# Attention and two mixtures of products on one core: base addresses of TensorE's operands moved by 32 bytes, and a new searched order

## The chip, the cores and the metric

One core of a Trainium2 chip runs the whole kernel as one program. The metric is the device time of that program in microseconds; shown are the median of several runs and, beside it, one profiled execution. The matmul engine is called PE in the profile, its weight loads PEld, VectorE DVE, ScalarE ACT, GpSimd POOL, and SyncE, which issues the DMAs, SP.

## The reference

Three stages follow each other. Everything is float32.

```python
# attention, B=4, H=8, S=576, D=64; key blocks of 64, block-causal
scores = where(block(i) >= block(j), q @ k.T / sqrt(D), -1e9)
attn   = exp(scores - max) ; attn /= attn.sum(-1) + 1e-9
x      = (attn @ v)                      # -> 2304 tokens x 512
# first mixture: 512 -> 1536 -> 512
xn = x / sqrt(mean(x*x) + 1e-6) * rms_g
x  = (silu(xn @ w_gate) * (xn @ w_val)) @ w_out
# second mixture: 8 experts, 512 -> 1024 -> 512
P  = exp(x @ gate - max), 8 rounds of row and column normalising
out = sum over e of P[:, e] * (relu(x @ w1[e]) @ w2[e])
```

## The kernel before, in words

**Products.** Nearly every product is made of three fp32r matmuls: each factor is split into a rounded part (`hi`, written by a copy) and the rest (`lo`, written by a subtraction), and hi·hi, hi·lo and lo·hi are added in PSUM (`THREE`). In a call `matmul(lhsT, rhs)` the stationary factor is `lhsT`, loaded as 128 columns, and the moving one is `rhs`, of up to 512 columns. In the rows of the trace a matmul is written `out<-moving,stationary`, so `ps<-xs,w` streams `xs` past weights from `w`.

**Stages.** In the first 500 us the 32 heads of attention are interleaved with the first mixture's products on the first three of five token blocks (`moe1`, `groups`). Some 12 heads (`NEW`) work with transposed scores, the other 20 turn their probabilities on PE (`tr`, 15 transposes a head, with `ident` moving and `p` stationary). Then the middle pass (`middle`) does token blocks 3 and 4 with 7 products in the place of 8 (Strassen's way, `up`), 384 columns wide. The first pass of the second mixture (`first_pass`) takes 10 of 18 token tiles, as pieces of 384 and 256 columns, the second pass (`second_pass`) the other 8 as one piece of 512. In the second pass each of 16 groups has 2 x 42 products with `xs` moving (`up`) and 84 with a tile of `h` or `x` moving (`down2`).

**Where operands lie.** SBUF tiles are laid one after another, each in a multiple of 32 bytes of a partition. The pool `cst` on the left begins with `ident` (512 bytes), `ones` (512) and `rgs` (16, rounded up to 32); by that all that follows (`acc`, the weights `w`, `raw`, `h`, `t`, the two big `x`) begins at 32 bytes modulo 64. On the right the pool `att` of attention (`qa`, `qb`, `ka`, `kb`, `vs`, `p`, `pth`, `ptl` and others) holds 78,624 bytes up to byte 229,344, so it begins at 150,720: its operands lie at 0 modulo 64. When the first tile of the later stages is wanted, `late` (L1166) closes that pool and opens `c1` in its place: seven operand tiles `xs`, the scratch tile `pad`, `gwr`, `onec`, the routing tables. Each is made when it is first asked for while instructions are written out, and this pool too begins at 150,720, so `xs` and `pad` lie at 0 modulo 64. All slices taken of these tiles begin at multiples of 64 bytes from the tile's start. `cst` ends at 150,688, so 32 bytes lie unused between them.

**Order.** Nothing is written in program order. `G.op` records each operation with an engine, a planned duration, buffers and a priority; `emit` (L136) plans them on a model of the engines forward and backward `ROUNDS` times, then `move` (L158) adds noise to the keys of stretches of the planned line, one stretch for each seed in `MOVES`, starting below position `SPAN`. What comes out is the order of each engine's queue. `MARGIN` is added to the time at which a finished operation is seen by other engines. Some operations can be given to a second engine (`alts`). `replay` (L268) finds gaps on PE and fills them with small matmuls of `ident` on itself (`Array.fill`, L84).

**Places the change touches.** Constants L24 to L337; `Loader.convert` (L486, two ACT operations); the pool `att` (L515 on); `att_init` (L564) with a memset of `ones` (L566) that releases PE's 32 warm-up products, and memsets of mask tiles (L578, L600); `att_load` (L622), `s_d` (L731), `s_norm` (L853, L858); `late` (L1166); the set `PRE` (L1273), which has the same nine members before and after.

Of the kernel before, what the change touches and what calls it, by code (L numbers as in the profile page):

```python
# [9 lines left out]
F32 = mybir.dt.float32  # L10
F32R = mybir.dt.float32r
I32 = mybir.dt.int32
U32 = mybir.dt.uint32
# [8 lines left out]


GAIN, GAIN2 = 1500.0, 3000.0  # L24
ROUNDS = 7


class Buf:
# [72 lines left out]
class Graph:  # L101
# [222 lines left out]

BEGIN = {"ACT": 700.0, "DVE": 900.0, "PE": 0.0, "POOL": 700.0, "SP": 740.0}
SEEN = {"ACT": 140.0, "DVE": 115.0, "POOL": 110.0, "PE": 210.0}
MARGIN, LAND, RATE = 0.0, 2000.0, 300.0
DELAY, BYTES = 1760.0, 307.0
FILL, EMPTY = 0.8, 220.0
MOVES = (  # L330
# [5 lines left out]
)  # L336
SPAN = 4502  # L337


def transfers(dur):  # L340
# [10 lines left out]
def t_act(n, psum=False, ap=0):  # L351
    return (50 if psum else 92) + n / 1.2 + 90 * ap
# [31 lines left out]
def tile_attn_moe_moe2(ctx: ExitStack, tc: tile.TileContext, qT, kT, vP, wg, wv, wo, rg, gw, w1, w2, ident_d, mq_d, mk_d, bm_d, out):  # L384
# [14 lines left out]
    def f32(ap):  # L399
        return ap.bitcast(F32)  # L400
# [60 lines left out]
    class Loader:  # L461
# [24 lines left out]
        def convert(self, src, raw, prio):  # L486

            wd, y, up = WIDE.next(), CVT[0].next(), CVT[1].next()

            def part(dt, i):  # L490
                return wd().bitcast(dt).rearrange("p (n w) -> p n w", w=2)[:, :, i]

            def i32(b):
                return b().bitcast(I32)

            ops = [
                G.op("SP", 2200, lambda: nc.sync.dma_start(out=wd().bitcast(U64), in_=src), w=[wd], prio=prio, lat=2000),

                G.op("ACT", t_act(512), lambda: nc.scalar.activation(out=y(), in_=part(F32, 1), func=AF.Prelu, scale=2.0**-112, alpha=2.0**32),
                     r=[wd], w=[y], prio=prio),  # L500
                G.op("ACT", t_act(512), lambda: nc.scalar.activation(out=i32(up), in_=part(U32, 0), func=AF.Copy, scale=2.0**-29),
                     r=[wd], w=[up], prio=prio),
                G.op("DVE", t_v2(512), lambda: nc.vector.tensor_scalar(
                    out=i32(y), in0=i32(y), scalar1=3, scalar2=None, op0=ALU.logical_shift_left), r=[y], w=[y], prio=prio),
                G.op("POOL", t_pool(512), lambda: nc.gpsimd.tensor_tensor(out=i32(raw), in0=i32(y), in1=i32(up), op=ALU.add),
                     r=[y, up], w=[raw], prio=prio),
            ]
            self.conv += ops
# [16 lines left out]
    PP = [Ring(tiles(att, 2, [128, 128 * (t + 1)], F32, f"p{t}_")) for t in range(5)]  # L525
    PTH = Ring(tiles(att, 2, [128, 512], F32R, "pth"))
    PTL = Ring(tiles(att, 2, [128, 512], F32R, "ptl"))
    MN = Ring(tiles(att, 2, [128, 6], F32, "mn"))
    SM = Ring(tiles(att, 2, [128, 5, 3], F32, "sm"))
    RS = Ring(tiles(att, 2, [128, 5], F32, "rs"))  # L530
    XX = Ring(tiles(att, 5, [128, S], F32, "xx"))
    SS = Ring(tiles(att, 1, [128, S], F32, "ss"))
    CL = Ring(tiles(att, 1, [128, 5], F32, "cl"))
    TM = Ring(tiles(att, 3, [128, S], F32, "tm"))
    guard, zeros = fixed(None), fixed(None, par=True)
    masks = {}

# [25 lines left out]

    def att_init():  # L564

        A("DVE", 200, lambda: nc.vector.memset(ones_t, 1.0), w=[ones], prio=-2.0)  # L566
        pt, first = PO.next(), RS.next()

        def warm():
            for _ in range(16):  # L570
                pe.matmul(out=pt()[:, 0:128], lhsT=ones_t, rhs=ones_t, start=True, stop=True)

        A("PE", 6800, warm, r=[ones], w=[pt], prio=-2.0)
        A("ACT", 1500, lambda: nc.scalar.activation(out=first()[:, 0:1], in_=ones_t[:, 0:1], func=AF.Exp), r=[ones], w=[first], prio=-2.0)
        m = [RQ0.next(), RQ0.next()]
        for b, src, ring, o in ((m[0], mq_d, QB0, PAD), (m[1], mk_d, KB0, 0)):
            def fill(b=b, one=ring is KB0):
                nc.vector.memset(b()[64:128], 0.0)  # L578
                if one:
                    nc.vector.memset(b()[96:106], 1.0)  # L580

            def rows(b=b, src=src):
                nc.sync.dma_start(out=b()[64:68], in_=src[0:4])
                nc.sync.dma_start(out=b()[68:72, PAD:S], in_=src[0:4, 0 : S - PAD])

            A("DVE", 1300 if ring is KB0 else 650, fill, w=[b])
            A("SP", 1150, rows, w=[b], lat=2000)
            for t in ring.tiles:
                masks[id(t)] = m_ = fixed(t, par=True)
                copy(A, S, lambda t=t, o=o: t[64:128, o : o + S], lambda b=b: b()[64:128], r=[b], w=[m_])  # L590
        A("SP", 300, lambda: nc.sync.dma_start(out=bm_t, in_=bm_d), w=[bm], lat=2000)
        for t in VX.tiles:
            A("POOL", 400, lambda t=t: nc.gpsimd.memset(t[:, :, 0:D], 1.0), w=[vones])
            A("POOL", 180, lambda t=t: nc.gpsimd.memset(t[0:64, 4, :], 0.0), w=[vones])
        for t in SM.tiles:
            A("DVE", 60, lambda t=t: nc.vector.memset(t, 0.0), w=[guard])
            A("DVE", 60, lambda t=t: nc.vector.memset(t[:, :, 1], 1e-9), r=[guard], w=[guard])
        for t in (*QA0.tiles, *QB0.tiles):
            m_ = masks.setdefault(id(t), fixed(t, par=True))
            A("DVE", 75, lambda t=t: nc.vector.memset(f32(t[:, 0:PAD]), 0.0), w=[m_])  # L600
        for t in range(5):
            for p in PP[t].tiles:
                A("POOL", 80, lambda t=t, p=p: nc.gpsimd.memset(p[:, NKEY[t] :], 0.0), w=[zeros])

    def att_load(i):
# [13 lines left out]
        if PLAIN <= i < PLAIN + 2:  # L619

            clear = st["clear", i % 2] = qb.part()
            A("DVE", 300, lambda: nc.vector.memset(f32(qb()[96:128, :]), 0.0), w=[clear])  # L622
        qq, kk = Rrq.next(), Rrq.next()
        load_two(kk, kT)
        load_two(qq, qT)
# [99 lines left out]
    def s_d(i):  # L725
        ps2, ps, m = st.pop(("s2", i)), ps_ring[0].next(), st["m", i]
        s_mm(i, ps, 0, 4, 512, 64)
        s_min(i, ps, 0, 5, 64)
        both = Buf(m.get)
        both.writes, both.before = set(m.writes), set()  # L730
        A("DVE", 70, lambda: nc.vector.tensor_scalar(  # L731
            out=m()[:, 4:5], in0=m()[:, 4:5], scalar1=m()[:, 5:6], scalar2=None, op0=ALU.min),
          w=[both], r=[m])
        m.writes |= both.writes
        m.users |= both.writes
        s_exp(i, ps2, 0, 4, 0, 0, 512)
        s_exp(i, ps, 0, 4, 512, 2, 64)
        if i in NEW:
            spread_max(i, ps)
# [104 lines left out]
    def s_norm(i):  # L844
        if i in NEW:
            return
        P, sm, r = st["P", i], st["sm", i], RS.next()

        def recip():
            nc.vector.tensor_reduce(out=r(), in_=sm(), axis=AX, op=ALU.add)  # L850
            nc.vector.reciprocal(out=r(), in_=r())

        A("DVE", 400, recip, r=[sm], w=[r])  # L853
        st["Pn", i] = []
        for t in range(5):
            n, p = NKEY[t], P[t]
            q = Buf(p.get)
            A("ACT", t_act(n), lambda t=t, n=n, p=p: nc.scalar.activation(  # L858
                out=p()[:, 0:n], in_=p()[:, 0:n], func=AF.Copy, scale=r()[:, t : t + 1]), r=[r, p], w=[q],
              alts=[("DVE", Both(63 + t_v2(n)), lambda t=t, n=n, p=p: nc.vector.tensor_scalar_mul(  # L860
                  out=p()[:, 0:n], in0=p()[:, 0:n], scalar1=r()[:, t : t + 1]))], margin=500.0)
            p.users |= q.users
            q.users = p.users
            st["Pn", i].append(q)
# [300 lines left out]

    def late(make):  # L1166

        box = []

        def get():  # L1170
            if not c_pool:
                att_stack.close()
                c_pool.append(ctx.enter_context(tc.tile_pool(name="c1", bufs=1, side="right", reuse_waits="tile")))
            if not box:
                box.append(make(c_pool[0]))
            return box[0]

        return get

    def late_buf(make, par=False):  # L1180
        b = Buf(late(make), par=par)
# [88 lines left out]
                    out=dst(), in0=ps()[:, 0:n], in1=dst(), op=ALU.add), r=[ps, dst], w=[dst])  # L1270

    kept, folded = {}, {}
    PRE = {('g', 1), ('g', 4), ('v', 1), ('g', 0), ('g', 3), ('v', 0), ('g', 5), ('v', 2), ('g', 2)}  # L1273

    def join(r, w, prio):
        hi, lo = (lambda: f32(w()[:, 0, :])), (lambda: f32(w()[:, 1, :]))
# [763 lines left out]
```

## Time and profile before

| | us |
|---|---|
| median of 3 runs (2166.33 to 2170.77) | 2166.95 |
| the profiled execution, its own time | 2168.07 |
| its span, first to last instruction | 2166.3 |
| PE busy | 2141.8 (99%) |
| PE weight loads | 1839.4 (85%) |
| DVE, POOL, ACT busy | 1510.9, 1192.0, 958.3 |

A matmul's record is longer than the time after which the next one starts, since they are pipelined; so the pace of PE is read from starts: a row of the timeline merges consecutive instructions of one kind, and its start subtracted from the start of the row behind it, divided by the count, is the pace. Busy time over count, in the groups by line, is close to it but counts the overlap once.

### The profile page before, as it was taken

Reading aid. Unit: us, or ns where it says so; the run is one execution under the profiler, and the core shown is the slowest. Engines: PE = TensorE matmul, PEld = TensorE weight load, DVE = VectorE, ACT = ScalarE, POOL = GpSimd, SP = SyncE. Lnnn points to the kernel's source line nnn. Section 1 sums busy time; section 2 is a strip of 40 time slices with the busy share of each in tenths; the row PEclk is TensorE's granted clock in tenths of the full one; section 3 lists DMA queues with packets and bytes.
Section 4 is the critical chain, followed back from the end, with each engine's and each line's share of the span. In section 5 each row is a group of like instructions: output and inputs, shape, how many; then the busy total and the mean of one; then the engine's idle time right before and its main releaser. Section 6 shows DMA issues by size and latency. Waiting matters only on the chain.

```text
span 2166.3 us, 31299 instructions
## 1 busy us (share of the span) xinstructions
PE 2141.8 (99%) x10924; PEld 1839.4 (85%) x10924; DVE 1510.9 (70%) x2576; ACT 958.3 (44%) x2055; POOL 1192.0 (55%) x1083
## 2 busy tenths in 40 slices
PE   8899999999999999999999999999999999999999
PEld 6777888888999889898999999989888888888887
DVE  8778886677556786666666656666767676776767
ACT  5668785663434434333333333433433233332332
POOL 4576424558436655555555555553655464564644
PEclk9999999999999999999999999999999999999999
DMA  5667754557654645555555544444766556565553
GB/s 170 204 209 240 240 181 155 178 183 268 236 170 148 214 176 201 187 185 188 182 182 183 177 178 175 175 177 163 238 199 209 181 194 208 190 211 188 194 197 114
DMA packets 166914, 414.39 MB, mean 191 GB/s; under 512 B 26378, under 2 KB 61642, under 8 KB 166756
## 3 DMA queue, kind: packets, MB, share of 16 engines
q1 hardware_dynamic: 166756, 412.39, 56.3%
q8 instruction: 86, 1.41, 0.3%
q14 instruction: 72, 0.59, 0.1%
HBM read 261.24 MB, written 150.53 MB: 190 GB/s over the span
## 4 chain that ended last, share of the span: by engine, by line
PE 91%; DVE 4%; ACT 3%; DMA 1%; issue 1%; POOL 0%; SPq 0%; ACTq 0%; DVEq 0%; POOLq 0%
PE pm L94 53%; PE ps L94 30%; PE po L94 5%; PE ps L98 1%; ACT p L858 1%; ACT p L697 1%; DVE mn L690 1%; PE pm L88 0%; ACT pth L874 0%; DMA kv<-w 0%; ACT tm L933 0%; DMA acc<-tm 0%; DVE ptl L875 0%; DMA w<-ko 0%; ACT w L443 0%
## 5 line engine op out<-in xcount | busy, mean ns | idle before, releaser
L94 PE MATMUL ps<-xs,w 128*128 128x384 f32 (+2 forms) x2613 | 536.3, 349 | 0.8 <-DVE pad L1501 0.8
L94 PEld LDWEIGHTS ps<-xs,w 128*128 128x128 f32 x2613 | 462.0, 188 | 54.4 <-DVE pad L1501 1.9
L94 PE MATMUL pm<-x,w 128*128 128x512 f32 (+2 forms) x1743 | 420.3, 375 | 2.0 <-DVE t L1244 1.1
L94 PEld LDWEIGHTS pm<-x,w 128*128 128x128 f32 x1743 | 306.8, 189 | 50.4 <-DVE t L1246 1.3
L1783 DVE SCALAR_TENSOR_TENSOR acc<-pm,Pm,acc 128x512 f32<-128x512 f32 x280 | 209.3, 748 | 114.9 <-PE pm L94 114.8
L94 PE MATMUL pm<-w,h 128*128 128x512 f32 x1152 | 280.4, 391 | 0.0
L456 POOL TENSOR_TENSOR w<-raw,w 128x512 fp32r<-128x512 f32 (+1 forms) x150 | 192.9, 1288 | 154.5 <-ACT w L443 143.8
L94 PE MATMUL pm<-h,w 128*128 128x512 f32 (+1 forms) x1068 | 248.6, 378 | 0.2 <-ACT x L443 0.2
L94 PEld LDWEIGHTS pm<-w,h 128*128 128x128 f32 x1152 | 209.7, 188 | 39.1
L94 PEld LDWEIGHTS pm<-h,w 128*128 128x128 f32 x1068 | 194.3, 188 | 30.1 <-ACT t L1496 0.6
L94 PE MATMUL pm<-w,x 128*128 128x512 f32 x768 | 192.8, 393 | 0.0
L1501 DVE TENSOR_TENSOR pad<-ps,pad 128x384 f32<-128x384 f32 (+2 forms) x154 | 81.2, 528 | 121.5 <-ACT pad L1496 87.1
L94 PEld LDWEIGHTS pm<-w,x 128*128 128x128 f32 x768 | 140.9, 188 | 24.9
L1496 ACT ACTIVATE pad<-ps 128x384 f32<-128x384 f32 (+2 forms) x142 | 68.1, 480 | 184.6 <-PE ps L94 183.5
L94 PE MATMUL pm<-xs,w 128*128 128x256 f32 (+2 forms) x699 | 149.7, 338 | 0.0
L1907 DVE TENSOR_TENSOR acc<-pm,acc 128x512 f32<-128x512 f32 x169 | 115.8, 686 | 45.2 <-PE pm L94 41.4
L443 ACT ACTIVATE w<-raw 128x512 fp32r<-128x512 f32 (+1 forms) x179 | 105.2, 590 | 91.6 <-PE pm L94 38.6
L94 PEld LDWEIGHTS pm<-xs,w 128*128 128x128 f32 x699 | 120.0, 188 | 16.7 <-DVE x L1738 0.4
L456 POOL TENSOR_TENSOR w<-pad,w 128x512 fp32r<-128x512 f32 x62 | 84.8, 1388 | 67.5 <-ACT w L443 41.6
L456 POOL TENSOR_TENSOR x<-pad,x 128x512 fp32r<-128x512 f32 (+1 forms) x74 | 99.8, 1352 | 32.8 <-ACT x L443 30.9
L94 PE MATMUL ps<-x,w 128*128 128x256 f32 (+1 forms) x627 | 114.3, 303 | 0.0
L456 POOL TENSOR_TENSOR h<-pad,h 128x512 fp32r<-128x512 f32 (+1 forms) x51 | 67.9, 1340 | 71.4 <-ACT h L443 43.3
(382 smaller groups left out, 3866.8 us busy)
## 6 DMA issues: line engine op xcount, KB each, us to landing
raw<-w_dram SPq DMA_DIRECT2D x128, 256.0 KB, 3.5
w<-ko SPq DMA_DIRECT2D x36, 512.0 KB, 4.5
w<-kv SPq DMA_DIRECT2D x33, 512.0 KB, 4.7
fa<-w SPq DMA_DIRECT2D x32, 512.0 KB, 2.6
fc<-w SPq DMA_DIRECT2D x32, 512.0 KB, 3.5
fd<-w SPq DMA_DIRECT2D x32, 512.0 KB, 3.1
sb<-w SPq DMA_DIRECT2D x32, 512.0 KB, 4.3
sd<-pad SPq DMA_DIRECT2D x32, 512.0 KB, 2.6
```

What stands on the lines that cost most here:

```text
L94: return self.tensor.matmul(**k)
L98: return self.tensor.transpose(**k)
L443: nc.scalar.activation(out=out_(), in_=in_(), func=AF.Copy, scale=scale)
L456: eng.tensor_tensor(out=out_(), in0=a(), in1=b(), op=ALU.subtract)
L690: return A("DVE", t_v1(n), lambda: nc.vector.tensor_reduce(out=m()[:, col : col + 1], in_=ps()[:, o : o + n], axis=AX, op=ALU.max, negate= ...
L697: A("ACT", t_act(n, True, 2), lambda: nc.scalar.activation(out=p()[:, c0 : c0 + n], in_=ps()[:, o : o + n], func=AF.Exp, bias=m()[:, t : t ...
L858: A("ACT", t_act(n), lambda t=t, n=n, p=p: nc.scalar.activation(out=p()[:, 0:n], in_=p()[:, 0:n], func=AF.Copy, scale=r()[:, t : t + 1]), ...
L1496: G.op("ACT", t_act(n, True), lambda: nc.scalar.activation(out=t()[:, 0:n], in_=bank()[:, 0:n], func=AF.Copy), r=[bank], w=[t])
L1501: G.op("DVE", t_v1(n), lambda: nc.vector.tensor_tensor(out=t()[:, 0:n], in0=bank()[:, 0:n], in1=t()[:, 0:n], op=ALU.add), r=[bank, t], w=[t])
L1783: G.op("DVE", 63 + t_v1(512), lambda y=y, dst=dst, tt=tt, e=e: nc.vector.scalar_tensor_tensor(out=dst(), in0=wide(y()), scalar=Pm()[:, tt, ...
L1907: G.op("DVE", t_v1(N), lambda: nc.vector.tensor_tensor(out=dst(), in0=bank()[:, 0:N], in1=dst(), op=ALU.add), r=[bank, dst], w=[dst])
```

## The change

Four things are changed together. The pool of attention gets one more tile of 32 bytes and, with that, its tiles `xx`, `ss`, `tm` stand ahead of the small ones. The late pool's tiles are all made at its opening, in a fixed order (`xs` 0 to 6, `pad`, `onec`, then `gwr`, `lg`, then the rest), and a tile of 32 bytes is added. Both pools thus hold 32 bytes more, and fill the 32 bytes that were free. Planned durations, `MARGIN` and `ROUNDS` are changed, and the list of moves is another, so the order on every engine is another. In `att_init` the memsets of masks are made to come behind the memset of `ones`.

```diff
-ROUNDS = 7
+ROUNDS = 9
-MARGIN, LAND, RATE = 0.0, 2000.0, 300.0
+MARGIN, LAND, RATE = 60.0, 2000.0, 300.0
 MOVES = (
...
-SPAN = 4502
+SPAN = 3975
...
-                G.op("ACT", t_act(512), lambda: nc.scalar.activation(out=y(), ...
+                G.op("ACT", 45 + t_act(512), lambda: nc.scalar.activation(out=y(), ...
-                G.op("ACT", t_act(512), lambda: nc.scalar.activation(out=i32(up), ...
+                G.op("ACT", 45 + t_act(512), lambda: nc.scalar.activation(out=i32(up), ...
...
     PTL = Ring(tiles(att, 2, [128, 512], F32R, "ptl"))
+    XX = Ring(tiles(att, 5, [128, S], F32, "xx"))
+    SS = Ring(tiles(att, 1, [128, S], F32, "ss"))
+    TM = Ring(tiles(att, 3, [128, S], F32, "tm"))
     MN = Ring(tiles(att, 2, [128, 6], F32, "mn"))
     SM = Ring(tiles(att, 2, [128, 5, 3], F32, "sm"))
     RS = Ring(tiles(att, 2, [128, 5], F32, "rs"))
-    XX = Ring(tiles(att, 5, [128, S], F32, "xx"))
-    SS = Ring(tiles(att, 1, [128, S], F32, "ss"))
     CL = Ring(tiles(att, 1, [128, 5], F32, "cl"))
-    TM = Ring(tiles(att, 3, [128, S], F32, "tm"))
+    att.tile([128, 8], F32, name="even")
...
-        A("DVE", 200, lambda: nc.vector.memset(ones_t, 1.0), w=[ones], prio=-2.0)
+        begun = {A("DVE", 200, lambda: nc.vector.memset(ones_t, 1.0), w=[ones], prio=-2.0)}
...
-            A("DVE", 1300 if ring is KB0 else 650, fill, w=[b])
+            A("DVE", 1300 if ring is KB0 else 650, fill, w=[b], after=begun)
...
-            A("DVE", 75, lambda t=t: nc.vector.memset(f32(t[:, 0:PAD]), 0.0), w=[m_])
+            A("DVE", 75, lambda t=t: nc.vector.memset(f32(t[:, 0:PAD]), 0.0), w=[m_], after=begun)
...
-            A("DVE", 300, lambda: nc.vector.memset(f32(qb()[96:128, :]), 0.0), w=[clear])
+            A("DVE", 750, lambda: nc.vector.memset(f32(qb()[96:128, :]), 0.0), w=[clear])
...
-        A("DVE", 70, lambda: nc.vector.tensor_scalar(
+        A("DVE", 135, lambda: nc.vector.tensor_scalar(
...
-        A("DVE", 400, recip, r=[sm], w=[r])
+        A("DVE", 300, recip, r=[sm], w=[r])
...
-            A("ACT", t_act(n), lambda t=t, n=n, p=p: nc.scalar.activation(
+            A("ACT", t_act(n, ap=1), lambda t=t, n=n, p=p: nc.scalar.activation(
...
     def late(make):
-        box = []
+        k = len(lates)
+        lates.append(make)
         def get():
             if not c_pool:
                 att_stack.close()
                 c_pool.append(ctx.enter_context(tc.tile_pool(name="c1", bufs=1, side="right", reuse_waits="tile")))
-            if not box:
-                box.append(make(c_pool[0]))
-            return box[0]
+                for i in (*range(2, 11), 0, 1, *range(11, len(lates))):
+                    lates[i] = lates[i](c_pool[0])
+                c_pool[0].tile([128, 8], F32, name="odd")
+            return lates[k]
         return get
+    lates = []
```

## Rows read from the trace of the kernel before

**Rows 1.** The page: share of the chain that ended last, by engine.

```profile
PE 91%; DVE 4%; ACT 3%; DMA 1%; issue 1%; POOL 0%; SPq 0%; ACTq 0%; DVEq 0%; POOLq 0%
```

**Rows 2.** Windows, first 500 us: length, busy of PE, PEld, DVE, ACT, POOL, clock, DMA.

```profile
0.00:60.00 60.00, 51.92 (x249) 39.80 (x249) 49.26 (x120) 36.01 (x75) 29.18 (x43) 0.91 0.60 172
60.00:125.00 65.00, 58.19 (x306) 47.87 (x307) 46.72 (x105) 43.05 (x98) 40.55 (x36) 0.95 0.58 176
125.00:250.00 125.00, 122.39 (x625) 97.48 (x624) 108.27 (x226) 95.13 (x231) 78.66 (x67) 1.00 0.76 244
250.00:500.00 250.00, 248.48 (x1309) 205.87 (x1308) 188.86 (x430) 164.98 (x423) 114.14 (x105) 1.00 0.58 187
```

**Rows 3.** Timeline of PE, second pass: start, length, form, count.

```profile
1709.40 2.88 PE L94 MATMUL pm<-x,w 128*128 128x512 f32 x12
1712.12 1.56 PE L94 MATMUL ps<-xs,w 128*128 128x512 f32 x6
...
1750.83 7.16 PE L94 MATMUL ps<-xs,w 128*128 128x512 f32 x30
1757.82 1.56 PE L94 MATMUL pm<-xs,w 128*128 128x512 f32 x6
```

**Rows 4.** Timeline of PE, first pass.

```profile
1058.28 5.42 PE L94 MATMUL ps<-xs,w 128*128 128x384 f32 x30
1063.54 1.55 PE L94 MATMUL pm<-w,x 128*128 128x512 f32 x6
```

**Rows 5.** Timeline of PE, middle pass.

```profile
596.11 7.44 PE L94 MATMUL pm<-h,w 128*128 128x384 f32 x42
603.39 1.20 PE L94 MATMUL ps<-x,w 128*128 128x384 f32 x6
...
608.60 1.20 PE L94 MATMUL ps<-xs,w 128*128 128x384 f32 x6
609.64 1.20 PE L94 MATMUL pm<-xs,w 128*128 128x384 f32 x6
```

**Rows 6.** Groups of PE by line and form, whole span: count, busy us, mean ns, idle.

```profile
L94 PE MATMUL ps<-xs,w 128*128 128x384 f32 x1383 | 262.0, 338 | 0.2 <-DVE pad L1501 0.2
L94 PE MATMUL ps<-xs,w 128*128 128x512 f32 x846 | 207.6, 395 | 0.0
...
L94 PE MATMUL pm<-xs,w 128*128 128x512 f32 x270 | 70.3, 395 | 0.0
...
L94 PE MATMUL ps<-xs,x 128*128 128x512 f32 x162 | 41.0, 395 | 0.0
...
L94 PE MATMUL pm<-xs,w 128*128 128x384 f32 x141 | 29.1, 339 | 0.0
...
L94 PE MATMUL pm<-xs,x 128*128 128x512 f32 x66 | 17.2, 396 | 0.0
```

**Rows 7.** Timeline of all engines, first 10 us.

```profile
3.00 0.17 DVE L566 MEMSET ones<- 128x128 f32 x1
...
3.22 5.88 PE L94 MATMUL po<-ones 128*128 128x128 f32 x32 [3.22 <-DVE ones L566]
...
7.25 0.75 DVE L640 TENSOR_TENSOR qa<-rq,qa 64x576 fp32r<-64x576 f32 x1
...
8.86 0.45 PE L94 MATMUL ps<-ka,qa 128*128 128x448 f32 x1
```

**Rows 8.** Timeline of all engines, the change from attention's tiles to the late pool.

```profile
521.16 1.43 DVE L1072 SCALAR_TENSOR_TENSOR acc<-xx,rgs,ss 128x64 f32<-128x64 f32 x3
521.27 1.05 POOL L1377 TENSOR_TENSOR pad<-acc,acc 128x384 f32<-128x384 f32 x1
...
542.28 1.32 PE L94 MATMUL ps<-x,w 128*128 128x384 f32 x6
```

**Rows 9.** Groups of PE by line and form, 0 to 500 us alone.

```profile
L94 PE MATMUL pm<-x,w 128*128 128x512 f32 x744 | 200.7, 403 | 2.0 <-DVE t L1244 1.1 <-DVE t L1246 0.8
```

**Rows 10.** One line's instructions: count, duration in ns as minimum, median, maximum.

```profile
L731 DVE TENSOR_SCALAR mn<-mn x32: 196/210/218, 13.9 to 465.4; 128x1 f32<-128x1 f32 x32
```

More of the change, by code (lines that the diff above doesn't have):

```diff
@@ L497, in convert @@
                 G.op("SP", 2200, lambda: nc.sync.dma_start(out=wd().bitcast(U64), in_=src), w=[wd], prio=prio, lat=2000),
-                G.op("ACT", t_act(512), lambda: nc.scalar.activation(out=y(), in_=part(F32, 1), func=AF.Prelu, scale=2.0**-112, alpha=2.0**32),
+                G.op("ACT", 45 + t_act(512), lambda: nc.scalar.activation(out=y(), in_=part(F32, 1), func=AF.Prelu, scale=2.0**-112, alpha=2.0**32),
                      r=[wd], w=[y], prio=prio),
-                G.op("ACT", t_act(512), lambda: nc.scalar.activation(out=i32(up), in_=part(U32, 0), func=AF.Copy, scale=2.0**-29),
+                G.op("ACT", 45 + t_act(512), lambda: nc.scalar.activation(out=i32(up), in_=part(U32, 0), func=AF.Copy, scale=2.0**-29),
                      r=[wd], w=[up], prio=prio),
@@ L1272, in tile_attn_moe_moe2 @@
     kept, folded = {}, {}
-    PRE = {('g', 1), ('g', 4), ('v', 1), ('g', 0), ('g', 3), ('v', 0), ('g', 5), ('v', 2), ('g', 2)}
+    PRE = {('g', 1), ('g', 4), ('g', 0), ('g', 3), ('v', 2), ('g', 2), ('v', 1), ('g', 5), ('v', 0)}
     def join(r, w, prio):
```

12 rows, old and new, of the table MOVES are left out of this document.

## The prediction

> **What bounds the kernel now.** I read the chain of waits first. The reader is to see that PE is 91% of the chain that ended last and no other engine has more than 4% [rows 1]: an instruction of PE that starts sooner brings the end nearer, anything else counts only where PE stands still. Where it does so is read from the windows. In the first 500 us PE is idle for 8.1, 6.8, 2.6 and 1.5 us, 19.0 in all [rows 2]; over the whole span it is 24.5 us (2166.3 less the 2141.8 of the table), so little is behind that. From 500 us on the time is the sum of the paces of PE's matmuls, so I read paces next, as starts in the timeline subtracted and divided by the count. In the second pass 12 products with `x` moving take 1712.12 - 1709.40 = 2.72 us, or 226.7 ns each; 30 with `xs` moving take 6.99 us, or 233.0 ns [rows 3]. Shape, weights and stage are the same. What differs is that `x` and `w` begin at 32 bytes modulo 64 and `xs` at 0, so that the moving and the stationary operand are of different classes in the second case. The same holds more weakly at 384 columns: 30 of `xs` in the first pass take 5.26 us, 175.3 ns [rows 4], 42 of `h` in the middle pass 7.28 us, 173.3 ns; but six of `xs` there take 1.04 us, also 173.3 ns [rows 5].
>
> **The change part by part.**
>
> *The late pool's base.* Before, it holds 78,624 bytes below byte 229,344; with 32 more it begins at 150,688, which is 32 modulo 64, and 8192 and 18432, the sizes of `xs` and `pad`, keep that class. All operands of the later passes are then of the class of `w`, `x` and `h`. The matmuls with `xs` moving and 512 columns number 846 + 270 + 162 + 66 = 1344 [rows 6]. If they go from 233.0 to 226.7 ns, 1344 x 6.3 = 8.5 us go, all from a stretch in which PE never waits, so all of it from the end. For 384 columns there are 1383 + 141 = 1524 [rows 6]. All at 2.0 ns would be 3.0 us; at the pace of the six in the middle pass it is nothing. I take 2.0 us, since two thirds or so of the 1524 lie in the first pass, where the slower pace was read. Products of 256 columns and the scratch operands in `pad` I leave at nothing, as no row parts them from the others. **-10.5 us**, between -11.5 and 0.
>
> *A rule that speaks against it.* The trace has 233.0 against 226.7 ns for the two classes [rows 3]. The Trainium skill, in "TensorE: Matmul & The Clock Gate", section "Step-by-step: what each phase is for", says that PE has two independent read ports into SBUF, one for the moving operand and one for weights, so that loading the next weights takes no bandwidth from the running matmul. By that rule the two bases could not collide, this term would be 0 and the time some 10.5 us longer. By the row I keep the term; the rule, taken at its word, is a rival below.
>
> *Attention's base.* Its operands move together from 0 to 32, so pairs within attention stay of one class; pairs at switches to and from products on `x` or `h`, mixed now, become equal, and the transposes, equal now, become mixed, since `ident` stays at 0 and `p` moves. No row isolates either. Bounds from the 6.3 ns of [rows 3]: some 200 switches give at most 1.3 us, 15 transposes in 20 heads lose at most 300 x 6.3 = 1.9 us. They stand against each other: **0**, between -1.3 and +1.9.
>
> *The memset of `ones` ahead.* Now DVE does five other memsets first; `ones` comes at 3.00 us, PE's warm-up starts at 3.22 us, runs for 5.88 us, and attention's first product starts right at its end, at 8.86 us [rows 7]. With `ones` first the warm-up is over up to 1.9 us sooner. What is late next is `qa`, whose split ends on DVE at 7.25 + 0.75 = 8.00 us [rows 7]. The memsets put behind cost DVE the 0.17 us of `ones` at most. **-0.7 us**, between -1.9 and 0.
>
> *The order of the late pool's tiles.* `pad` now lies over attention's `xx`, `ss` and `tm`, which are read last. The release waits on DVE: POOL's first write of `pad` at 521.27 us would wait until DVE's last reads of `xx` and `ss` end at 522.59 us [rows 8], 1.3 us, and POOL's folding of weights, queued behind it, with it. The first product that needs operands made through `pad` starts at 542.28 us [rows 8]. These 20 us, in which PE works on pending products of the first mixture, hide it: **0**; were that cover gone, 1.3 us.
>
> *The new order.* Removed and added instructions: none; each queue's order is another, in the first 500 us above all, SP's and POOL's included. One row says in which direction: the operation of L731, on the path from scores to exponentials, takes 210 ns 32 times [rows 10], and was planned with 70, now with 135. A plan that knows more of what the chip takes, and keeps 60 ns in hand at each handover, should stall less. What there is to win has two rows: the 19.0 us of idle [rows 2], of which 3.2 are the wait for `ones`, and the pace of the first mixture's products on `x` where attention is mixed in, 200.7 / 744 = 269.8 ns against 226.7, or 744 x 43.1 = 32 us [rows 9, 3]. Most of that slow pace is the price of switching to small products and back, which any order pays. What there is to lose is as large: an order can as well double the idle time. Between -15.8 (all idle but the wait for `ones`) and +19.0 (idle doubled) I take **-3.0 us**, near the small end, as both orders come from the same kind of search.
>
> **Sum.** -10.5 + 0 - 0.7 + 0 - 3.0 = -14.2 us. It stands against the profiled execution's own 2168.07 us, 1.8 us of which lie around the span: 2153.9 us. That execution is 1.1 us above the median of 2166.95 us, so the median should go to **2152.8 us**.
>
> **Rivals.**
>
> *The bases do nothing.* Either the ports are as separate as the cited rule has them and `xs` is slow for another reason, say because it lies highest in SBUF or is written while it is read; or the pool's base is rounded to 64 and the shift never happens. For it: six of `xs` run at 173.3 ns beside `x` and `h` [rows 5]. Against it: at 512 columns `xs` is slow in the second pass, where it is only read, and the rest of the pass is not [rows 3]. Then -0.7 - 3.0 remain: 2166.95 - 3.7 = 2163.3 us.
>
> *The new order does much.* If it saves a third of the 32 us of slow pace, some 10.7 us in the place of 3.0, the time is 2152.8 - 7.7 = 2145.1 us. For it: DVE is busy 108.27 of 125 us between 125 and 250 us [rows 2], so PE there waits on handovers that an order can move. Against it: the idle time in that window is 2.6 us.
>
> *The new order starves PE, and the kernel is slower.* The place is that same window: with DVE at 87% [rows 2], 60 ns of planned slack at each handover puts attention's chain of maximum, exponential and transpose later, and products of the first mixture run out before it is done. Doubled idle time costs 19.0 us: 2166.95 - 10.5 - 0.7 + 19.0 = 2174.8 us. It decides from the point at which PE's idle in the first 500 us passes 19.0 + 11.2 + 4.3 = 34.5 us. Against it: PE has 744 products on `x` alone to put in [rows 9].
>
> **How the numbers follow.** 0.2% is 4.3 us, about what a measurement of this kernel can tell from no change. Chances: the forecast 0.63, the order doing much 0.17, the bases doing nothing 0.11, the starved PE 0.09. The first two are faster by more than 4.3 us, and so is a small part of the third, if the order gives a little more: 0.81. The third otherwise, and some of the fourth, are within: 0.11. Slower: 0.08. The forecast's own terms reach from about 2144 to 2162 us; the range takes in most of the second rival and the third case, and leaves out the starved PE and the far end of the order's gain: 2141 to 2164 us.
>
> **What would show it.** In the timeline of the second pass, `xs` moving at about 227 ns where it had 233.0, in runs of 12 or more, and `h` and `x` as before; at 384 columns in the first pass 173 to 174 ns. If these stay, the first step is wrong and the first rival right. The warm-up should start before 2 us and attention's first product near 8.1 us. PE's idle in the four windows of the first 500 us should be 10 to 20 us; over 34 us is the slow rival. The first write of `pad` may come after DVE's last read of `xx`, with no idle on PE behind it. The prediction is wrong as a whole if the stretch behind 500 us gives back less than 7 us, or if the first 500 us grow by more than they shrink.

## The result and the profile after

| | before | after |
|---|---|---|
| median of the runs (lowest to highest) | 2168.01 us (2166.33 to 2170.77, 4 runs) | 2141.0 us (2140.24 to 2145.28, 4 runs) |
| ratio, 95% interval | | 0.9878 [0.9861, 0.9896] |
| profiled execution, its span | 2168.07 us, 2166.3 us | 2140.24 us, 2138.4 us |

The kernel is 27.0 us (1.2%) faster, where 14.2 were forecast: it lies on the low bound of the range, 2141 us, past the rival in which the order does much.

PE still sets the end: it is 93% of the chain that ended last, DVE 3%, against 91% and 4% in [rows 1].

**The later passes.** Timeline of PE, second pass: start, length, form, count.

```profile
1712.09 2.88 PE L94 MATMUL pm<-x,w 128*128 128x512 f32 x12
1714.81 1.52 PE L94 MATMUL po<-x,w 128*128 128x512 f32 x6
...
1729.77 6.96 PE L94 MATMUL ps<-xs,w 128*128 128x512 f32 x30
1736.57 1.52 PE L94 MATMUL pm<-xs,w 128*128 128x512 f32 x6
```

Thirty products with `xs` moving now take 1736.57 - 1729.77 = 6.80 us, 226.7 ns each, where [rows 3] has 233.0; `x` keeps 226.7. Timeline of PE, first pass:

```profile
1069.50 1.23 PE L94 MATMUL ps<-xs,w 128*128 128x384 f32 x6
1070.57 1.20 PE L94 MATMUL pm<-xs,w 128*128 128x384 f32 x6
1071.61 3.28 PE L94 MATMUL ps<-xs,w 128*128 128x384 f32 x18
1074.73 0.63 PE L94 MATMUL pm<-w,x 128*128 128x512 f32 x2
```

These 30 take 5.23 us, 174.3 ns each, against 175.3 in [rows 4] and the 173 to 174 named as a sign. How much a whole pass gains is read from how many matmuls go through in equal stretches where PE never waits. Windows of the kernel before (length, busy and count of PE, PEld, DVE, ACT, POOL, then clock, DMA share, GB/s):

```profile
900.00:1480.00 580.00, 580.00 (x3193) 523.70 (x3192) 357.33 (x553) 227.97 (x486) 331.61 (x335) 1.00 0.51 181
1540.00:2130.00 590.00, 590.00 (x2572) 480.88 (x2571) 418.38 (x542) 193.02 (x317) 320.74 (x220) 1.00 0.59 197
```

The same of the kernel after:

```profile
900.00:1480.00 580.00, 580.00 (x3210) 524.72 (x3209) 320.32 (x533) 228.06 (x493) 347.21 (x356) 1.00 0.52 183
1540.00:2130.00 590.00, 590.00 (x2614) 488.71 (x2614) 436.96 (x558) 194.52 (x318) 326.50 (x223) 1.00 0.59 194
```

In the second pass 42 more matmuls fit into 590 us; at 590 / 2614 = 0.226 us each that is 9.5 us. In the first pass 17 more fit into 580 us, 3.1 us. The two stretches are the same in time, not quite in the work they cut out, so these are sizes, not exact sums. That the 17 are not the shift's work, the experiments show.

**The first 500 us.** The first product of the middle pass started at 542.28 us [rows 8]. Timeline of the kernel after:

```profile
529.16 1.23 PE L94 MATMUL ps<-x,w 128*128 128x384 f32 x6
```

It starts 13.1 us sooner. Windows of the kernel after, to be laid beside [rows 2]:

```profile
0.00:60.00 60.00, 55.39 (x285) 42.02 (x286) 53.92 (x129) 38.12 (x86) 30.48 (x46) 1.00 0.66 182
60.00:125.00 65.00, 55.31 (x292) 44.95 (x291) 53.70 (x105) 41.72 (x91) 44.99 (x37) 0.97 0.61 190
125.00:250.00 125.00, 121.86 (x634) 99.90 (x633) 109.21 (x237) 95.19 (x232) 79.60 (x70) 1.00 0.80 247
250.00:500.00 250.00, 248.96 (x1329) 210.79 (x1329) 196.58 (x430) 162.30 (x414) 126.86 (x109) 1.00 0.61 197
```

PE's idle is 4.61 + 9.69 + 3.14 + 1.04 = 18.5 us, against 19.0. So the 13.1 us did not come from idle, as the records count it. The groups of PE in 0 to 500 us say what filled them, first one of the kernel before:

```profile
L94 PE MATMUL pm<-h,w 128*128 128x512 f32 x343 | 88.4, 398 | 0.0
```

The kernel after:

```profile
L94 PE MATMUL pm<-x,w 128*128 128x512 f32 x784 | 211.4, 405 | 3.1 <-DVE x L1040 2.7 <-DVE t L1251 0.3
...
L94 PE MATMUL pm<-h,w 128*128 128x512 f32 x360 | 91.8, 397 | 0.0
```

There are 40 more products on `x` than in [rows 9] and, against 343 of them before, 17 more on `h`: 57 products of the first mixture more in the same 500 us, at the same busy time for each (211.4 / 784 = 269.6 ns against 269.8). That figure is not the pace, since the last record of every run counts in full; from one start to the next these products on `x` take 248.7 ns before and 252.4 after. Attention and what goes with it left PE that much more time. One part of this stands in a column that the prediction passed over, the granted clock. Windows of 10 us, kernel before:

```profile
10.00:20.00 10.00, 8.00 (x31) 6.13 (x30) 9.52 (x22) 3.01 (x7) 2.27 (x3) 0.72 0.86 238
...
40.00:50.00 10.00, 7.84 (x31) 4.92 (x30) 6.01 (x13) 5.57 (x13) 5.95 (x6) 0.83 0.62 207
```

The same two of the kernel after:

```profile
10.00:20.00 10.00, 8.77 (x46) 5.85 (x45) 9.72 (x25) 4.65 (x12) 2.75 (x4) 1.00 0.88 235
...
40.00:50.00 10.00, 10.00 (x51) 7.16 (x49) 7.74 (x16) 8.14 (x21) 6.20 (x5) 1.00 0.69 204
```

A value below 1.00 is a mean over a stretch at 2.4 GHz and one at 1.2. Before, the clock fell four times in the first 125 us; after, once, at 100 to 110 us. How often it falls differs from execution to execution (two to five times in the first 250 us with the old order, one to three with the new), but the first fall does not: between 10 and 20 us the clock is 0.66 to 0.76 in all five profiled kernels with the old plan and 1.00 in all nine with the new one. What PE did ahead of the first fall (the clock is 1.00 up to 14 us and 0.50 from 15 to 21 us), timeline of the kernel before:

```profile
9.15 0.37 PE L94 MATMUL ps<-kb,qb 96*128 96x448 f32 x1
...
12.31 0.47 PE L94 MATMUL ps<-qa,ka 128*128 128x448 f32 x1 [1.13 <-DVE mn L690]
...
14.76 0.71 PE L94 MATMUL ps<-kb,qb 96*128 96x448 f32 x1 [0.77 <-POOL acc L747]
```

The kernel after, the same stretch:

```profile
12.16 0.47 PE L94 MATMUL ps<-qa,ka 128*128 128x448 f32 x1 [0.25 <-DVE mn L693]
12.57 1.04 PE L88 MATMUL pm<-ident 128*10 128x128 f32 x8
...
16.04 0.49 PE L94 MATMUL pm<-qb,kb 128*128 128x512 f32 x1 [0.81 <-DVE qb L756]
```

Before, a stall of 1.13 us stands ahead of the fall, and the fall comes within a second one of 0.77 us, from 13.99 to 14.76 us. After, other scores fill the first, eight of the planner's filler products stand at 12.57 us, one stall of 0.81 us comes later, and the clock stays at 2.4 GHz. That the stalls are the cause is not shown: new_plan_bare, below, has stalls of 0.79 and 1.10 us there and keeps 1.00 as well.

**Start and handover.** Timeline of all engines, kernel after, first 10 us:

```profile
0.83 0.17 DVE L569 MEMSET ones<- 128x128 f32 x1 [0.83 <-PEq L2037]
1.05 6.41 PE L94 MATMUL po<-ones 128*128 128x128 f32 x32 [1.05 <-DVE ones L569]
...
7.51 0.47 PE L94 MATMUL ps<-ka,qa 128*128 128x448 f32 x1
8.57 0.44 PE L94 MATMUL ps<-kb,qb 96*128 96x448 f32 x1 [0.59 <-DVE kb L449]
```

The warm-up starts 2.2 us sooner and the first product 1.35 us sooner than in [rows 7], but the second waits for `kb`: at 8.57 us it is only 0.58 us ahead of the 9.15 us of before. Handover to the late pool:

```profile
502.81 0.67 DVE L1075 SCALAR_TENSOR_TENSOR acc<-xx,rgs,ss 128x64 f32<-128x64 f32 x3
...
504.13 1.25 DVE L1384 TENSOR_TENSOR pad<-acc,acc 128x384 f32<-128x384 f32 x1
```

The first write of `pad` now comes behind the last read of `xx`, and 25 us ahead of the product at 529.16 us: covered, as forecast.

### The profile page after: what moved, and what is told of

Read it like the earlier page. It is cut to its first block, busy times and chain, and to the rows that moved or that the text cites. A ratio compares the mean times of both kernels' runs of the same rounds, so it can differ in the third digit from the quotient of the medians.

```text
span 2138.4 us, 31268 instructions
## 1 busy us (share of the span) xinstructions
PE 2115.0 (99%) x10906; PEld 1833.8 (86%) x10906; DVE 1484.8 (69%) x2551; ACT 951.5 (44%) x2052; POOL 1220.3 (57%) x1111
## 4 chain that ended last, share of the span: by engine, by line
PE 93%; DVE 3%; DMA 2%; ACT 1%; issue 0%; SPq 0%; POOL 0%; DVEq 0%; POOLq 0%; ACTq 0%
PE pm L94 55%; PE ps L94 31%; PE po L94 5%; PE ps L98 2%; DMA acc<-wg_dram 1%; DVE mn L693 1%; DMA w<-kg 0%; DMA x<-rd 0%; DMA rd<-acc 0%; DMA acc<-wv_dram 0%; DVE qb L449 0%; DVE xx L844 0%; DVE ss L959 0%; DVE qa L451 0%; DVE qb L756 0%
## 5 line engine op out<-in xcount | busy, mean ns | idle before, releaser
L94 PE MATMUL ps<-xs,w 128*128 128x384 f32 (+2 forms) x2613 | 527.7, 345 | 0.0
L458 POOL TENSOR_TENSOR w<-raw,w 128x512 fp32r<-128x512 f32 (+1 forms) x178 | 214.9, 1216 | 111.2 <-ACT w L445 94.0
L94 PE MATMUL pm<-w,x 128*128 128x512 f32 x768 | 186.9, 392 | 0.0
L458 POOL TENSOR_TENSOR x<-pad,x 128x512 fp32r<-128x512 f32 (+1 forms) x65 | 89.6, 1380 | 48.7 <-ACT x L445 48.1
L1503 ACT ACTIVATE t<-ps 128x384 f32<-128x384 f32 (+1 forms) x72 | 36.2, 503 | 176.8 <-PE ps L94 176.8
```

The lines of the kernel that those rows point to most:

```text
L94: return self.tensor.matmul(**k)
L458: eng.tensor_tensor(out=out_(), in0=a(), in1=b(), op=ALU.subtract)
L1503: G.op("ACT", t_act(n, True), lambda: nc.scalar.activation(out=t()[:, 0:n], in_=bank()[:, 0:n], func=AF.Copy), r=[bank], w=[t])
```

## The experiments

The times below are medians; the ratio is to the kernel before on the same chip, whose median there was 2168 to 2169 us.

**The layout alone, and the rest without the shift.** shift_only is the kernel before with the change's layout of both pools, the shift by 32 bytes and the fixed order of the late tiles together:

```diff
+    XX = Ring(tiles(att, 5, [128, S], F32, "xx"))
+    SS = Ring(tiles(att, 1, [128, S], F32, "ss"))
+    TM = Ring(tiles(att, 3, [128, S], F32, "tm"))
...
+    att.tile([128, 8], F32, name="even")
...
+                for i in (*range(2, 11), 0, 1, *range(11, len(lates))):
+                    lates[i] = lates[i](c_pool[0])
+                c_pool[0].tile([128, 8], F32, name="odd")
```

> Before's plan, moves and order, with both pools' layouts of the changed kernel (all operands but ident and ones at 32 modulo 64). If the pace follows from equal classes of the moving and stationary operand, or from the class 32 by itself: xs moving at 226.7 ns in the second pass where before had 233.0, and the time 10 to 12 us under before's (ratio 0.9945 to 0.9955). If the bases do nothing and all came from the order: before's time, xs at 233.

2157.56 us, ratio 0.9953 [0.994, 0.9965]: 11.4 us. Timeline, second pass:

```profile
1751.27 6.96 PE L94 MATMUL ps<-xs,w 128*128 128x512 f32 x30
1758.07 1.52 PE L94 MATMUL pm<-xs,w 128*128 128x512 f32 x6
```

The 30 take 6.80 us, 226.7 ns, with the old order around them. order_only is the kernel after without both tiles of 32 bytes, so that the bases lie at 0 modulo 64; the late tiles keep their fixed order:

```diff
-    att.tile([128, 8], F32, name="even")
...
-                c_pool[0].tile([128, 8], F32, name="odd")
```

> The changed kernel without its two tiles of 32 bytes, so that both pools begin at 0 modulo 64 again; its order is kept. If bases and order add up: about 15 to 17 us under before (ratio 0.992 to 0.993), xs at 233 ns in the second pass. If the bases do nothing: the changed kernel's time, 27 us under before (0.988).

2152.55 us, ratio 0.9925 [0.9913, 0.9937]: 16.4 us. Timeline, second pass:

```profile
1703.06 2.96 PE L94 MATMUL ps<-xs,w 128*128 128x512 f32 x12
1705.86 1.56 PE L94 MATMUL ps<-xs,x 128*128 128x512 f32 x6
```

Twelve take 2.80 us, 233.3 ns: `xs` is slow as before. 11.4 + 16.4 = 27.8, the whole is 27.0: the parts add up, and what comes with the new order is the larger one.

Two readings inside the profiled executions say where each part lies. Windows of the first pass, shift_only, then order_only:

```profile
900.00:1480.00 580.00, 580.00 (x3191) 522.74 (x3190) 357.39 (x556) 228.21 (x486) 329.76 (x332) 1.00 0.51 182
900.00:1480.00 580.00, 580.00 (x3209) 525.73 (x3208) 321.24 (x533) 227.95 (x491) 346.55 (x356) 1.00 0.52 182
```

Before has 3193: the shift adds nothing here, and the 17 more of the kernel after come with the order, which also puts more products of 256 columns and fewer of 384 into this stretch. First product of the middle pass, shift_only, then order_only:

```profile
546.78 1.33 PE L94 MATMUL ps<-x,w 128*128 128x384 f32 x6
530.22 1.22 PE L94 MATMUL ps<-x,w 128*128 128x384 f32 x6
```

From there to the end of the span before takes 1624.0 us, shift_only 1613.7, order_only 1619.6 and the kernel after 1609.2. So the shift's gain, 10.3 us, lies behind this point; its later start, 546.8 against 542.3 us, is that of the slowest of its five executions, in which the clock fell five times. Of order_only's, 4.4 us lie behind it and 12.1 ahead. Whether the 4.4 are the order's or the fixed tile order's no run parts.

**Attention's base.** late_shift leaves out the tile `even` alone, so attention's operands are at 0.

> The changed kernel without the tile in attention's pool alone: attention's operands at 0, the late pool's at 32. If attention's base is worth nothing or its gain at switches and its loss at transposes stand against each other, the changed kernel's time within 1.5 us (ratio to before 0.987 to 0.989). If mixed pairs in the first 500 us matter, 1.5 us or more above it.

after_again is the kernel after, run once more beside the experiments.

> The changed kernel itself, for a comparison on the same chip: ratio to before 0.987 to 0.989, 2140 to 2143 us.

2142.27 us, ratio 0.9884 [0.987, 0.9897]. The kernel after had 2141.0 and as after_again 2141.68 us, ratio 0.9877 [0.9864, 0.9891]: attention's base is worth no more than these runs can tell.

**Is it the class 32, or that all classes are equal?** all_zero is the kernel before with a tile of 32 bytes ahead of the tiles of the constants' pool, which brings `w`, `x` and `h` to 0, where `xs` already was:

```diff
+    cst.tile([128, 8], F32, name="step")
```

> Before's order with 32 bytes put into the left pool ahead of the accumulators, so that all operands of all stages lie at 0 modulo 64. If equal classes make the pace: as the kernel with the shift alone, 10 to 12 us under before, with xs, x and h all near 226.7 ns in the second pass. If the class 32 by itself is the fast one: x, h and w fall to 233 ns too, and the time is over before's, by 8 us in the second pass alone. If the bases do nothing: before's time.

2161.13 us, ratio 0.9967 [0.9956, 0.9978]: 7.8 us, less than the 11.4. Timeline, second pass:

```profile
1709.42 4.32 PE L94 MATMUL ps<-xs,x 128*128 128x512 f32 x18
1713.58 2.91 PE L94 MATMUL ps<-xs,w 128*128 128x512 f32 x12
```

The 18 take 4.16 us, 231.1 ns: between the two paces. The late tiles are still laid as they are first asked for. By their starts, the first `xs` has 226.7 ns, the second 228.5 and the other five 230.1 to 231.7; two of these five lie 64 off from `w` modulo 512. The other three and the second lie 1024 off a multiple of 2048, the first at a multiple of it. zero_fixed adds the fixed order of the late tiles, without the tile `odd`, which puts every `xs` at a multiple of 2048 from `w`:

```diff
+                for i in (*range(2, 11), 0, 1, *range(11, len(lates))):
+                    lates[i] = lates[i](c_pool[0])
```

> The kernel with all operands at 0 and, in addition, the late pool's tiles in the fixed order of the changed kernel, so that every xs lies a multiple of 2048 bytes from w, as it does in the kernel with the shift alone. If the distance between the two operands is what counts: all xs at 226.7 ns in the second pass, and the time of the shift alone, ratio 0.994 to 0.9965. If the class 32 is faster by itself: xs at about 230 ns again, ratio 0.9965.

2156.8 us, ratio 0.9945 [0.9932, 0.9959], the same as shift_only.

```profile
1710.69 4.24 PE L94 MATMUL ps<-xs,x 128*128 128x512 f32 x18
1714.77 2.88 PE L94 MATMUL ps<-xs,w 128*128 128x512 f32 x12
```

The 18 take 4.08 us, 226.7 ns. order_only has its `xs` at these same addresses and `w` 32 bytes off, and 233.3 ns. So it is how the operands lie to each other, not the class 32, and the fixed order has a part of its own, 2161.13 - 2156.8 = 4.3 us between two chips, 3.6 with each taken against before on its own chip. Two kernels then move `xs`, and `pad` behind it, in the kernel after, by 512 bytes (lead_512) and by 576, which is 64 modulo 512 (lead_576):

```diff
-                for i in (*range(2, 11), 0, 1, *range(11, len(lates))):
+                for i in (10, *range(2, 10), 0, 1, *range(11, len(lates))):
```

> The changed kernel with onec laid ahead of the xs tiles, so that xs and pad move up by 512 bytes: still 32 modulo 64, but 512 bytes off a multiple of 2048 from w. If the class modulo 64 is all that counts: xs stays at 226.7 ns, ratio to before 0.9877 as the changed kernel. If the distance counts in a larger unit: xs between 227 and 234 ns, as the xs tiles of the kernel with all at 0 that lay 1024 off, and 3 to 9 us over the changed kernel.

```diff
-                for i in (*range(2, 11), 0, 1, *range(11, len(lates))):
+                for i in (1, *range(2, 11), 0, *range(11, len(lates))):
```

> The changed kernel with lg laid ahead of the xs tiles: they move up by 576 bytes, still 32 modulo 64, 64 bytes off a multiple of 512 from w. If the class modulo 64 is all that counts: 226.7 ns and the changed kernel's time. If the distance counts in a larger unit: xs between 229 and 236 ns, as xs3 and xs5 of the kernel with all at 0, and 4 to 10 us over the changed kernel.

lead_512: 2142.4 us, ratio 0.9881 [0.9868, 0.9895], `xs` at 226.7 ns: 512 bytes change nothing. lead_576: 2142.52 us, ratio 0.9884 [0.9868, 0.99]: not the 4 to 10 us over the kernel after that were expected, as two things cancel. Timeline, second pass, then windows:

```profile
1730.02 7.05 PE L94 MATMUL ps<-xs,w 128*128 128x512 f32 x30
1736.91 1.54 PE L94 MATMUL pm<-xs,w 128*128 128x512 f32 x6
```

```profile
900.00:1480.00 580.00, 580.00 (x3226) 526.56 (x3225) 322.35 (x537) 228.37 (x494) 348.08 (x356) 1.00 0.52 184
1540.00:2130.00 590.00, 590.00 (x2591) 485.13 (x2590) 434.20 (x553) 193.39 (x316) 325.98 (x222) 1.00 0.58 192
```

The 30 take 6.89 us, 229.7 ns, and 23 matmuls fewer than after fit into the second pass; but 16 more fit into the first. first_64 tries to keep both: in the first pass alone the slices of `xs` lie 64 bytes later. The seven `xs` are one block, 64 bytes longer, so that `pad` behind it lies 64 bytes later too, and the run does not part the two.

```diff
...
-                        o = (2 * k + c) * n
+                        o = (2 * k + c) * n + 16 * (p == 0)
...
-                        o = 4 * WIDTH[p][0] + c * n
+                        o = 4 * WIDTH[p][0] + c * n + 16 * (p == 0)
...
-        onec = late_buf(lambda p: p.tile([128, 128], F32, name="onec"))
+        onec = late_buf(lambda p: ones_t)
```

> The changed kernel with the seven xs laid as one block, whose slices begin 64 bytes later in the first pass than in the second (the middle pass 512 bytes later), onec sharing the memory of ones to make room. From the kernel with xs 576 bytes up, whose first pass was 3.3 us shorter and second pass 4.6 us longer: the first pass shorter by 3 us, the second as in the changed kernel, so 2138 us, 3 us under the changed kernel. If the first pass of that kernel was shorter because pad had moved too: the changed kernel's time.

```profile
900.00:1480.00 580.00, 580.00 (x3223) 526.42 (x3222) 321.99 (x537) 228.08 (x493) 348.43 (x357) 1.00 0.52 184
1540.00:2130.00 590.00, 590.00 (x2614) 488.55 (x2613) 437.54 (x557) 193.92 (x318) 326.81 (x223) 1.00 0.59 194
```

Both windows are as meant: 13 more in the first pass, some 2.3 us, and the second as after. But the whole is 2141.38 us, ratio 0.9875 [0.9862, 0.9888]: no gain that these runs can tell from the kernel after. In its profiled execution the middle pass starts at 532.15 us, 3.0 us later than after, with a clock of 0.92 in place of 0.97 between 60 and 125 us; from there to the end it takes 1605.7 us, 3.5 less than the kernel after.

ident_too lays `rgs` first among the constants, so that `ident` and `ones` come to 32 like the rest:

```diff
+    rg_t = cst.tile([128, NK], F32, name="rgs")
...
-    rg_t = cst.tile([128, NK], F32, name="rgs")
```

> The changed kernel with rgs laid first in the left pool, so that ident and ones lie at 32 modulo 64 as well and nothing else moves. If mixed classes cost a transpose what they cost a product of 512 columns: up to 1.9 us under the changed kernel, and in one look no more than a start of the first 384-column product sooner by that. If a transpose of 128 columns is bound by its weight load: the changed kernel's time within 1 us.

2141.56 us, ratio 0.9876 [0.9863, 0.989]: nothing. What the transposes lose by the class of `ident` is not seen.

**What in the order does it?** old_plan_bare is the kernel before, new_plan_bare the kernel after, each with its table of moves empty, so that the planner's own order runs:

```diff
 MOVES = (
-    22000004, 22000041, 22000050, 22000065, 22000131, 22000140, 22000157, 22000176, 22000177, 22000181, 22000191,
...
 )
```

> Before with an empty list of moves, so the order is the plan's own. If the moves of before earned something on the chip, it is slower than before by what they earned, 5 to 20 us; bases as before, xs at 233 ns.

> The changed kernel with an empty list of moves. If the 16 us of the order come from the new durations, margin and rounds: about 27 us under the bare plan of before, 11 of them from the bases. If they come from the longer list of moves: only about 11 us under the bare plan of before, and 16 us or more over the changed kernel beyond what before's own moves earned.

old_plan_bare: 2167.66 us, ratio 0.9997 [0.9989, 1.0006]. The 53 old moves earned nothing on the chip; the 5 to 20 us expected were a miss. new_plan_bare: 2152.16 us, ratio 0.9931 [0.9918, 0.9945], between the two cases that were expected. So of the 27 us some 11 are the layout, 5 the new durations, margin and rounds with the memset of `ones`, and 2152.16 - 2141.68 = 10.5 the 70 new moves.

In new_plan_bare the clock falls to 0.66 between 40 and 50 us, where the kernel after has 1.00, and to 0.66 between 100 and 110 us, where it has 0.83. What that costs can be read from the runs of the kernel before beside these experiments: 19 with a mean granted clock of 0.995 average 2169.6 us, 14 with 0.996 average 2167.7, so 1.8 us for each 0.001. The mean clock was 0.9946 without the new moves and 0.9978 with them, which answers to 3.2 x 1.8 = 5.8 of their 10.5 us; in order_only it was 0.998 against 0.9955 before, 2.5 x 1.8 = 4.5 of its 16.4 us. In shift_only it was 0.995, no higher than before: the gain of the bases owes nothing to the clock. No edit changed the clock alone, so this share rests on how the runs vary, and is not shown by itself. One run stands against stretching it: of the kernel after's four, the one of 2145.28 us has a mean clock of 0.947 on record and is only some 5 us longer than the others.

## Why the prediction was right in part

*The late pool's base*, -10.5: right in the sum, with luck in its parts. shift_only measured -11.4, `xs` went from 233.0 to 226.7 ns, and order_only without it kept 233.3. The 512 columns carry more than the 8.5 forecast: behind the last product of 384 or 256 columns shift_only takes 632.8 us and before 642.7. The 2.0 taken for 384 columns are not there: from the first product of the middle pass to that last one it takes 980.9 us, before 981.3. In the first pass of shift_only, by their starts, products of 384 columns went from 176.4 to 175.4 ns and those of 256 on `xs` from 119.7 to 118.6, but those of 256 on `x` from 118.4 to 120.0. The 11.4 hold the fixed order of the late tiles too; equal classes with the tiles laid as before gave 7.8 (all_zero). The rule of two independent read ports (the Trainium skill, "TensorE: Matmul & The Clock Gate", section "Step-by-step: what each phase is for") would have made this term 0; the trace does not agree, since where the moving operand lies against the stationary one sets a pace of 226.7, 229.7 or 233 ns with the same shapes. The rival built on it has fallen, and so has my own reason in part: being of one class modulo 64 is not enough (all_zero). At 64 off modulo 512 `xs` is slower (lead_576); but in all_zero slices at 1024 bytes off a multiple of 2048 are slow too, so the whole rule of the distances is not found.

*Attention's base*, 0: right, as far as these runs can tell. *The memset of `ones`*, -0.7: right at its place, where the second product comes 0.58 us sooner; no run has it alone. I had named `qa` as the next to be late; `qa` is in time and `kb` is late. *The late tiles' order*, 0 for the release at the handover: right. That it also sets the distances of `xs` was not seen; zero_fixed puts some 4 us on it when everything lies at 0.

*The new order*, -3.0: the term that failed, by its size. order_only measured -16.4, with some -0.6 of `ones` in it, which leaves -15.8 with what the fixed tile order does in it, where -3.0 was taken. That it equals the outermost bound given is chance, since that bound was PE's idle. The step that failed is "what there is to win has two rows", idle and the pace of products on `x`. Idle stayed (19.0 to 18.5) and the busy time of a product stayed (269.8 to 269.6). The second row was misread as well: 269.8 ns is not a pace, and from start to start, 248.7 against 226.7 ns, some 16 us lay there and not 32. A third source stood in the same [rows 2], the clock: 60 x 0.09 + 65 x 0.05 = 8.7 us of full clock were missing, and 65 x 0.03 = 2.0 are missing after. Of the rest, some 12 us by the sum above, 4.4 lie behind the start of the middle pass. The other 7 or so are attention's small products and transposes taking less of PE between them, so that, with the clock's part, 57 more products of the mixture fit. It is not fewer switches: in the first 500 us PE changes between products of the mixture and other work 331 times before and 339 after. Shorter waits are seen in one place: within runs of transposes the median from start to start is 109 ns both times, the mean 121.7 before and 113.6 after, some 1.6 us in all. A transpose's record lasts some 280 ns, so such waits do not show as idle. Fewer filler products are another small part, 76 for 94. How the rest divides stays open. The reason for the small end, "both orders come from the same kind of search", is refuted: the old moves earn 0, the new 10.5 us.

The rival in which the order does much had the right direction, 2145.1 us, and the wrong mechanism: the slow pace it drew on did not get better. The rival of a starved PE was far off: the idle did not grow. That the time still fell into the range, on its bound, is luck: the range had been drawn wide enough for that rival, and the term that moved most was sized at a fifth.

## What to carry to other kernels

Where PE never waits, read the pace of each pair of moving and stationary tiles from runs of starts; if the same shape has two paces, look at the addresses of the two tiles against each other, and fix the order in which a pool lays its tiles, or the distances are left to chance. Where an order is to be judged, count products per stretch and read the granted clock beside the idle: an order can win 16 us with the idle unchanged, and a wait that is shorter than a record's overlap with the next is not counted as idle. And measure a search's moves with the table emptied: of the two tables here one was worth 10.5 us on the chip and the other nothing.

## What the runs showed of the hardware that was not expected

With the late tiles in a fixed order, a product of 512 columns takes 226.7 ns with `xs` at 0 or 512 bytes beyond a multiple of 2048 from `w` (shift_only, lead_512), 229.7 at 576 (lead_576) and 233.3 at 32 (order_only).

A move of `xs`, and of `pad` behind it, changes the pace of products that read neither. Timeline of PE, first pass of the kernel after, where products of 256 and 512 columns alternate:

```profile
1059.12 1.55 PE L94 MATMUL pm<-w,h 128*128 128x512 f32 x6
1060.50 0.52 PE L94 MATMUL pm<-xs,w 128*128 128x256 f32 x3
```

The same in lead_576:

```profile
1059.72 1.52 PE L94 MATMUL pm<-w,h 128*128 128x512 f32 x6
1061.08 0.52 PE L94 MATMUL pm<-xs,w 128*128 128x256 f32 x3
...
1061.79 1.55 PE L94 MATMUL pm<-w,h 128*128 128x512 f32 x6
1063.18 0.52 PE L94 MATMUL pm<-xs,w 128*128 128x256 f32 x3
```

Six products on `w` and `h` take 1.38 us after, and in lead_576 1.36 us in one place and 1.39 in another. Starts one by one show why the sums differ. In the kernel after, behind 256 columns the first five of 512 take 233, 236, 228, 233 and 231 ns on average, and then the pace settles at 226.7; in lead_576 the first five take 229, 230, 227, 229 and 228. What inside PE or SBUF does this was not settled.
